# Two neighbouring products of a block change places in TensorE's order

## The chip, the cores and the metric

The kernel runs on one core of a Trainium2 chip. The metric is the device time of one execution in microseconds (us); a kernel's time is the median of its runs.

## The reference

Linear attention with decay over two batches of eight heads, 768 positions and 64 values a head, then two MLPs without bias, one after the other, on the 1536 tokens by 512 values that the attention leaves. All of it in float32:

```
h = x @ w_in                      # 512 -> 2048
g = h * clip(h + 3, 0, 6) / 6     # first MLP;  second MLP: max(0.01 * h, h)
x = g @ w_out                     # 2048 -> 512
```

## The kernel before, in words

The 1536 tokens are three **tiles** of 512 (t = 0, 1, 2). The 2048 hidden values of an MLP are sixteen **slices** of 128 (f = 0 to 15). The work of an MLP is cut into steps (l, b, t, f): MLP, block, tile, slice. `BLOCKS` says how many slices a block has: 1, 3, 4, 4, 4 in the first MLP. Within a block the kernel goes through tile 0 with all slices, then tile 1, then tile 2.

A number is held as a high and a low part (`wh`, `wl`; `xh`, `xl`; `Gh`, `Gl`), and each product is three matmuls: high by high, high by low, low by high.

- **First product** (`gemm1`, L610, called by `one`): 12 matmuls give h of one tile and one slice in a PSUM bank (`h`, of which there are two, for the slices of the first two blocks; `a`, also two, for later ones).
- **Gate** (`gates`): ScalarE L619 (ReLU), VectorE L623 (the product with h, which frees the bank), ScalarE L629 (`Gh`), VectorE L636 (`Gl`).
- **Second product** (`gemm2`, L698): G times the slice of `w_out`, four quarters e = 0 to 3 of 3 matmuls each, summed over the slices of the block in the PSUM banks `acc0` to `acc3` (tile 1 of the first two blocks uses `a` for e = 0 and 1).
- **Collection** of the four banks when a block's last slice of a tile is through (`collect`): in the first MLP's second and third blocks, e = 0, 1 and 2 are copied by ScalarE to a staging buffer `st` (L709), and GpSimd issues a DMA that adds it to the sums in SBUF (L653); e = 3 is added by VectorE (L711). There are two `st` buffers, so the third copy waits until the first of these DMAs has landed, and the bank `acc2` is held until that copy is done.

Weights come in as raw 64-bit values, 512 KB for one slice of one matrix (DMA issued by SyncE, L158; three buffers `raw`). ScalarE (L495, L499) and VectorE (L506 to L521) make float32 of them, ScalarE L527 the high part, VectorE L531 the low part. L518 reads `raw` last, and a new load starts when it is through.

From the third block on, tiles 0 and 1 and two neighbouring slices are multiplied by seven products (`product`, L786, 6 matmuls each) in place of eight, from sums of weights (`s`) and sums of tokens (`T1` to `T4`). Their results are kept and joined by ScalarE L827 and VectorE L831; the join L831 of the third result also frees the second of the two `h` banks.

All operations are entered with `add`, each with what it comes after, which buffers it takes and frees, an assumed duration for each engine and a due time. `Order.issue` walks through assumed time and starts whatever is ready, the one with the lowest due time first, when its engine and buffers are free; this fixes the order of the instructions on each engine for good. First products have due times `due1`, a step of 5.45 apart in the order of the steps; each one is also entered as coming after the one that was entered before it (`prev1`). On the chip, each engine works through its fixed order and waits on semaphores.

Of the kernel before, what the change touches and what calls it, by code (L numbers as in the profile page):

```python
# [131 lines left out]
def decay_attention_two_mlps(ctx: ExitStack, tc: tile.TileContext, qkk, vv, lam, w1, w2, out):  # L132
# [33 lines left out]
    starts = [[sum(bs[:i]) for i in range(len(bs) + 1)] for bs in BLOCKS]  # L166
# [5 lines left out]
    at_step = {(l, t, f): s for s, (l, b, t, f) in enumerate(steps)}  # L172
# [12 lines left out]
    due1 = [T_FIRST + T_STEP * s for s in range(NS)]  # L185
# [162 lines left out]
    def scores_bank(u, g):  # L348
        def fn(e):
            PA["s", u, g] = new("pair", [P, 2, HG, SBT], F32)  # L350
            scores(u, g)(e)
        return fn
# [57 lines left out]
    for u in range(NSB):  # L410
        d, last = DUE_S + SBT_STEP * u, u + 1 == NSB
# [5 lines left out]
    def piece(name, fn, **kw):  # L417
        pieces[name] = add(("pe", PE_US[name[0]]), fn, due_pe[name], **kw)
        return pieces[name]
# [8 lines left out]
    for u in range(NSB):  # L428
        d, last = DUE_S + SBT_STEP * u, u + 1 == NSB
# [11 lines left out]
        for g in range(2):  # L441
            s = piece(("s", u, g), scores_bank(u, g), after=[ld["q", u], ki, op_warm], takes=["pair"])
# [438 lines left out]
    def second_end(ss):  # L881
        nonlocal prev2

        def go(s, e, at, n=None):
            nonlocal prev2
            l, b, t, f = steps[s]
            first, last = f == starts[l][b], f + 1 == starts[l][b + 1]
            bank = "h" if n else f"acc{e}"
            prev2 = add(("pe", 0.68 if n is None else 0.34), gemm2(s, e) if n is None else gemm2_half(s, n), at,
                        after=[gate[s][0], w_ready[l, f, 1], prev2], takes=[bank] * first)  # L890
            if not last:
                return
            cs = slice(0, TT) if n is None else half_of(n)
            c = add(("dve", 0.69 if n is None else 0.42), collect(s, e) if n is None else collect_half(t, n), at,
                    after=[prev2, *taken[t, e]])
            add(("dma", 0.75), store(t, e, cs), at, after=[c])

        places = [(e, None) for e in range(3)] + [(3, 0), (3, 1)]
        for s in ss[:2]:
            for e, n in places:  # L900
                go(s, e, due2[s], n)
            add(("none", 0.0), nothing, after=[prev2], frees=["G", "w1"])
        for group in (places[:2], *([x] for x in places[2:])):
            for s in ss[2:]:
                for e, n in group:
                    go(s, e, due2[ss[3]], n)

    n1, n0 = starts[0][SINGLE] * NTT, NS // 2
# [43 lines left out]
    def one(s, after):  # L952
        nonlocal prev1
        l, b, t, f = steps[s]
        h = "a" if paired(l, f) else "h"
        g1 = add(("pe", 2.73), gemm1(s), due1[s], after=[w_ready[l, f, 0], prev1, *after],
                 takes=[h] + ["G"] * (h == "h"), frees=["w0"] * (t == NTT - 1 and h == "h"))
        last1[l, t] = prev1 = g1
        pieces["m", s] = g1
        gates(s, [g1], h)  # L960
        return g1
# [74 lines left out]
    def seconds(l, b):  # L1036
        for s in range(NS):
            if ends(s):
                continue
            if steps[s][:2] == (l, b):  # L1040
                if steps[s][2] == 2 and steps[s][3] == starts[l][b] and l == 0 and b + 1 == len(BLOCKS[0]):
                    sums_pair()
                sums = second(s, gate[s][0], [gate[s][1]] + ["w1"] * (steps[s][2] == NTT - 1))
                if sums and b + 1 == len(BLOCKS[l]):
                    sums_of[l, steps[s][2]] = sums
        if (l, b) == (1, len(BLOCKS[1]) - 1):
            second_end([s for s in range(NS) if ends(s)])

    x_of = lambda t: [x_ready[c] for c in range(t * SPT, (t + 1) * SPT)]
    for b in range(SINGLE):  # L1050
        for s in range(n1):
            if steps[s][1] == b:
                one(s, x_of(steps[s][2]))
        seconds(0, b)
# [191 lines left out]
```

## Time and profile before

| | before |
|---|---|
| median of 3 runs | 553.12 us (552.95 to 554.85) |
| the profiled execution | 553.77 us |
| its span, first to last instruction | 552.0 us |
| TensorE busy | 543.7 us, 98% of the span |
| VectorE busy | 421.6 us, 76% |
| ScalarE busy | 347.2 us, 63% |
| mean of all DMA | 106 GB/s |

The profiled execution has 1.8 us outside its span, and is 0.65 us above the median. Shares of busy time are means over stages that differ: VectorE is busy 19.48 of the 20 us from 60 to 80, and 164.34 of the 246 us from 300 to 546. The granted TensorE clock is 1.00 in every stretch.

### The profile page before, as it was taken

The numbers are of one execution on the slowest core, as the hardware profiler recorded it, in microseconds if no ns is written. First come the engines' busy times: TensorE is split into PE (matmuls) and PEld (weight loads), VectorE is DVE, ScalarE is ACT, GpSimd is POOL, SyncE is SP. The second block draws the span as 40 slices with busy tenths as digits, with TensorE's granted clock in tenths as the row PEclk, the third lists the DMA queues.
The fourth block names the chain that finished last, engine by engine and source line by source line (L and its number), as shares of the span: only waits on it lengthen the run. The fifth ranks groups of instructions, "written<-read, shape, count | busy, mean of one in ns | idle before, by whom it ended". The sixth has DMA issues, their size and how long they took to land.

```text
span 552.0 us, 8352 instructions
## 1 busy us (share of the span) xinstructions
PE 543.7 (98%) x3174; PEld 457.0 (83%) x3174; DVE 421.6 (76%) x711; ACT 347.2 (63%) x629; POOL 55.7 (10%) x62
## 2 busy tenths in 40 slices
PE   9899999999999999999999999999999999999996
PEld 5788878888888888888888888888888888888885
DVE  4778999899898986888789798786477953883342
ACT  3766976578567754587767796686258735574220
POOL 1680001110110100110000000000110110010000
PEclk9999999999999999999999999999999999999999
DMA  8993333545455323432210411341333522321323
GB/s 284 354 329 143 113 117 57 125 113 145 86 124 172 78 58 86 106 127 64 78 39 1 126 65 44 110 154 38 77 76 115 148 63 53 84 53 23 77 66 88
DMA packets 22571, 58.75 MB, mean 106 GB/s; under 512 B 2690, under 2 KB 2946, under 8 KB 22530
## 3 DMA queue, kind: packets, MB, share of 16 engines
q1 hardware_dynamic: 16944, 48.24, 26.7%
q0 software_dynamic: 5184, 9.44, 10.2%
q8 instruction: 25, 0.41, 0.3%
q10 hardware_dynamic: 402, 0.52, 0.3%
q14 instruction: 16, 0.13, 0.1%
HBM read 45.61 MB, written 3.15 MB: 88 GB/s over the span
## 4 chain that ended last, share of the span: by engine, by line
PE 90%; DMA 5%; DVE 2%; ACT 1%; SPq 0%; issue 0%; ACTq 0%
PE acc L698 45%; PE h L786 21%; PE a L786 14%; PE h L610 5%; DMA sums<-qkk 4%; PE a L610 2%; PE a L698 1%; DMA qk<-qkk 1%; PE pair L345 1%; PE h L395 1%; SPq L158 0%; DVE x_spare L772 0%; ACT ki L318 0%; PE a L387 0%; PE h L387 0%
## 5 line engine op out<-in xcount | busy, mean ns | idle before, releaser
L653 POOL DMA_DIRECT2D sums<-st x36 | 31.8, 933 | 422.0 <-ACT st L709 416.5
L698 PE MATMUL acc<-Gh,wh 128*128 128x512 f32 x136 | 53.1, 390 | 0.0
L698 PE MATMUL acc<-Gl,wh 128*128 128x512 f32 x136 | 53.1, 390 | 0.0
L698 PE MATMUL acc<-Gh,wl 128*128 128x512 f32 x136 | 52.9, 389 | 0.0
L698 PE MATMUL acc<-wh,Gh 128*128 128x512 f32 x124 | 48.5, 391 | 0.0
L698 PE MATMUL acc<-wl,Gh 128*128 128x512 f32 x124 | 48.5, 391 | 0.0
L698 PE MATMUL acc<-wh,Gl 128*128 128x512 f32 x124 | 48.2, 389 | 0.0
L495 ACT ACTIVATE c<-raw 128x512 uint32<-128x512 uint32 x64 | 43.1, 675 | 7.1 <-DVE t L521 5.1
L521 DVE CUSTOM_DVE_ANT_0 t<-t,c 128x1024 uint16<-128x1024 uint16 x64 | 44.3, 692 | 2.2
L711 DVE TENSOR_TENSOR sums<-acc,sums 128x512 f32<-128x512 f32 x35 | 24.1, 690 | 28.3 <-PE acc L698 28.1
L531 DVE TENSOR_TENSOR wl<-t,wh 128x512 fp32r<-128x512 f32 (+1 forms) x64 | 41.9, 659 | 4.0 <-ACT wh L527 3.9
L518 DVE SCALAR_TENSOR_TENSOR t<-raw,t 128x512 uint32<-128x512 uint32 x64 | 44.0, 688 | 1.0
L499 ACT ACTIVATE t<-raw 128x512 f32<-128x512 f32 x64 | 42.8, 668 | 0.0
L527 ACT CAST wh<-t 128x512 fp32r<-128x512 f32 (+1 forms) x64 | 37.7, 591 | 3.0 <-PE acc L698 2.3
L786 PE MATMUL h<-xh,s 128*128 128x512 f32 x112 | 38.4, 389 | 0.0
L506 DVE TENSOR_SCALAR t<-t 128x512 f32<-128x512 f32 x64 | 27.0, 422 | 12.9 <-ACT t L499 12.9
L639 DVE TENSOR_TENSOR Gl<-u,Gh 128x512 fp32r<-128x512 f32 x32 | 22.1, 690 | 17.8 <-ACT Gh L836 17.5
L842 ACT ACTIVATE u<-a 128x512 f32<-128x512 f32 x24 | 14.4, 598 | 29.1 <-PE a L786 29.1
L709 ACT COPY st<-acc 128x512 f32<-128x512 f32 x34 | 19.8, 586 | 18.5 <-PE acc L698 16.2
L698 PEld LDWEIGHTS acc<-Gh,wl 128*128 128x128 f32 x136 | 25.5, 188 | 5.4
L698 PEld LDWEIGHTS acc<-Gh,wh 128*128 128x128 f32 x136 | 25.6, 188 | 4.9
L698 PEld LDWEIGHTS acc<-Gl,wh 128*128 128x128 f32 x136 | 25.6, 188 | 4.9
(210 smaller groups left out, 1478.0 us busy)
## 6 DMA issues: line engine op xcount, KB each, us to landing
raw<-w SPq DMA_DIRECT2D x58, 512.0 KB, 3.3
sums<-st POOLq DMA_DIRECT2D x36, 256.0 KB, 3.8
sums<-qkk SPq DMA_DIRECT2D x12, 256.0 KB, 4.8
vs<-vv SPq DMA_DIRECT2D x12, 256.0 KB, 5.2
sums<-qkk SPq DMA_DIRECT2D x6, 512.0 KB, 5.6
raw<-w SPq DMA_DIRECT2D x12, 256.0 KB, 4.0
out<-sums SPq DMA_DIRECT2D x19, 128.0 KB, 2.4
qk<-qkk SPq DMA_DIRECT2D x4, 512.0 KB, 5.7
```

The costliest lines, as they stand in the source:

```text
L495: nc.scalar.activation(out=CV[h][1], in_=RAW[h][:, :, 0], func=AF.Copy, scale=2.0 ** -29)
L499: return lambda _: nc.scalar.activation(out=CV[h][0].bitcast(F32), in_=RAW[h][:, :, 1].bitcast(F32), func=AF.Abs)
L506: nc.vector.tensor_scalar(out=t.bitcast(F32), in0=t.bitcast(F32), scalar1=MAG_MIN, scalar2=MAG_MAX, op0=ALU.max, op1=ALU.min)
L518: nc.vector.scalar_tensor_tensor(out=t, in0=RAW[h][:, :, 1], scalar=0xC0000000, in1=t, op0=ALU.bitwise_and, op1=ALU.bitwise_or)
L521: nc.vector.tensor_tensor(out=t, in0=t, in1=c, op=ALU.add)
L527: nc.scalar.copy(out=W[h][0][:, cols(*h)], in_=CV[h][0].bitcast(F32)[:, cols(*h)])
L531: return lambda e: eng[e].tensor_tensor(out=W[h][1][:, cols(*h)], in0=CV[h][0].bitcast(F32)[:, cols(*h)], in1=W[h][0].bitcast(F32)[:, cols ...
L610: mm(ps, a[:, ws], x[:, k, :], start=(n == 0), stop=(n == 3 * KC - 1))
L653: return lambda _: nc.gpsimd.dma_start(out=SUM[t][:, e, :], in_=STAGE[t, e], accum_op=ALU.add)
L698: mm(ACC[e], a, x, start=(first and n == 0 and not seeded(s, e)), stop=(last and n == 2), skip_group_check=seeded(s, e))
L711: nc.vector.tensor_tensor(out=acc, in0=ps, in1=acc, op=ALU.add)
L786: mm(ps, ws[a][:, c * P:(c + 1) * P], xs[b][:, c], start=(first and n == 0), stop=(n == 5), skip_group_check=True)
```

## The change

Before the first products of the first two blocks are entered, their list is altered: the step of tile 1 and the block's first slice (l, b, t, f = 0, 1, 1, 1) goes ahead of the step of tile 0 and the block's third slice (0, 1, 0, 3). The due times of first products are dealt out anew to the list, so that the moved step gets the place and the due time of the other. Second products keep their due times and the order in which they are entered.

```
     x_of = ...
+    turns = list(range(n1))
+    other_tile, third_slice = at_step[0, 1, starts[0][1]], at_step[0, 0, starts[0][1] + 2]
+    turns.insert(turns.index(third_slice), turns.pop(turns.index(other_tile)))
+    for s, d in zip(turns, [due1[s] for s in range(n1)]):
+        due1[s] = d
...
     for b in range(SINGLE):
-        for s in range(n1):
+        for s in turns:
             if steps[s][1] == b:
                 one(s, x_of(steps[s][2]))
         seconds(0, b)
```

No instruction is added or taken away: TensorE has the same matmuls. The order differs on TensorE, VectorE and ScalarE from here into the fourth block; behind that it is the same.

On TensorE at the place of the edit, behind the first product of tile 0 and the second slice (its last matmuls are the first three rows; `xh_120` is tile 0, `xh_122` is tile 1), there stood the second products of the block's first slice:

```order
L610 MATMUL h<-xh_120,wh 128x512
L610 MATMUL h<-xl_121,wh 128x512
L610 MATMUL h<-xh_120,wl 128x512
L698 MATMUL acc_1006<-Gh,wh 128x512
L698 MATMUL acc_1006<-Gl,wh 128x512
```

and there stands now the first product of tile 1 and the first slice:

```order
L610 MATMUL h<-xh_120,wh 128x512
L610 MATMUL h<-xl_121,wh 128x512
L610 MATMUL h<-xh_120,wl 128x512
L610 MATMUL h<-xh_122,wh 128x512
L610 MATMUL h<-xl_123,wh 128x512
```

The second products follow it, and then comes the first product of tile 0 and the third slice, one first product later than before.

On TensorE at the start of the fourth block, the second products of its first slice (e = 0 is `acc_2112`, e = 1 is `acc_2119`) were followed by the second of the seven products of the next pair (`T10h`):

```order
L698 MATMUL acc_2119<-Gh,wh 128x512
L698 MATMUL acc_2119<-Gl,wh 128x512
L698 MATMUL acc_2119<-Gh,wl 128x512
L786 MATMUL h<-T10h,s 128x512
L786 MATMUL h<-T10l,s 128x512
```

Now e = 2 (`acc_2125`, in the bank `acc2`) stands between e = 1 (`acc_2111`) and that product; before, e = 2 came four products later:

```order
L698 MATMUL acc_2111<-Gh,wl 128x512
L698 MATMUL acc_2125<-Gh,wh 128x512
L698 MATMUL acc_2125<-Gl,wh 128x512
L698 MATMUL acc_2125<-Gh,wl 128x512
L786 MATMUL h<-T10h,s 128x512
```

On ScalarE at the same place, these rows stood behind the second staging copy of the third block's last tile, and the last of them is the third staging copy, which frees `acc2`:

```order
L629 ACTIVATE Gh<-u 128x512
L527 CAST wh<-t 128x512
L1098 CAST x<-x 128x512
L827 COPY a<-h 128x512
L499 ACTIVATE t<-raw 128x512
L619 ACTIVATE u<-ux,three 128x512
L1098 CAST xh_124<-x 128x2x256
L827 COPY ux<-h 128x512
L629 ACTIVATE Gxh<-u 128x512
L827 COPY ux<-h 128x512
L1098 CAST x<-x 128x512
L709 COPY st<-acc_1923 128x512
```

Now the three staging copies stand so, the third with six rows ahead of it behind the second:

```order
L709 COPY st<-acc_1905 128x512
L495 ACTIVATE c<-raw 128x512
L709 COPY st<-acc_1913 128x512
L629 ACTIVATE Gh<-u 128x512
L499 ACTIVATE t<-raw 128x512
L527 CAST wh<-t 128x512
L827 COPY a<-h 128x512
L495 ACTIVATE c<-raw 128x512
L499 ACTIVATE t<-raw 128x512
L709 COPY st<-acc_1954 128x512
```

On VectorE at the same place, L518, behind which the next weight load starts, stood ahead of the gate L623, and the join L831 was three rows behind the collection L711:

```order
L518 SCALAR_TENSOR_TENSOR t<-raw,t 128x512
L521 ISA t<-t,c 128x1024
L531 TENSOR_TENSOR wl<-t,wh 128x512
L756 TENSOR_TENSOR x<-x 128x512
L623 SCALAR_TENSOR_TENSOR u<-u,h 128x512
L756 TENSOR_TENSOR x<-x 128x512 x2
L711 TENSOR_TENSOR sums<-acc_1929,sums 128x512
L636 SCALAR_TENSOR_TENSOR Gl<-u,Gh 128x512
L531 TENSOR_TENSOR wl<-t,wh 128x512
L831 TENSOR_TENSOR ux<-h,ux 128x512
```

Now L518 stands behind L623, and the join is five rows behind L711:

```order
L623 SCALAR_TENSOR_TENSOR u<-u,h 128x512
L518 SCALAR_TENSOR_TENSOR t<-raw,t 128x512
L521 ISA t<-t,c 128x1024
L711 TENSOR_TENSOR sums<-acc_1962,sums 128x512
L636 SCALAR_TENSOR_TENSOR Gl<-u,Gh 128x512
L756 TENSOR_TENSOR x<-x 128x512
L531 TENSOR_TENSOR wl<-t,wh 128x512
L756 TENSOR_TENSOR x<-x 128x512
L831 TENSOR_TENSOR ux<-h,ux 128x512
```

## Rows read from the trace of the kernel before

**Rows 1.** The page: busy time, share of the span and instructions of each engine
```profile
PE 543.7 (98%) x3174; PEld 457.0 (83%) x3174; DVE 421.6 (76%) x711; ACT 347.2 (63%) x629; POOL 55.7 (10%) x62
```

**Rows 2.** Busy time by stretch: stretch, length, PE, PEld, DVE, ACT, POOL, clock, DMA
```profile
80.00:180.00 100.00, 100.00 (x443) 82.78 (x442) 91.18 (x151) 69.33 (x115) 13.21 (x15) 1.00 0.48 119
180.00:200.00 20.00, 20.00 (x89) 16.25 (x88) 19.72 (x35) 14.38 (x25) 2.59 (x3) 1.00 0.31 67
200.00:546.00 346.00, 345.93 (x1765) 295.69 (x1764) 247.01 (x426) 209.11 (x375) 15.99 (x18) 1.00 0.28 77
```

**Rows 3.** TensorE's timeline, second block: start, duration, operation, idle before it
```profile
71.36 0.39 PE L610 MATMUL h<-xh,wh 128*128 128x512 f32 x1
71.58 0.39 PE L610 MATMUL h<-xl,wh 128*128 128x512 f32 x1
72.20 0.50 PE L610 MATMUL h<-xh,wl 128*128 128x512 f32 x1 [0.23 <-DVE wl L531]
72.53 0.39 PE L610 MATMUL h<-xh,wh 128*128 128x512 f32 x1
...
74.60 0.39 PE L698 MATMUL acc<-Gh,wh 128*128 128x512 f32 x1
```

**Rows 4.** VectorE's timeline, the low parts of two slices' weights
```profile
71.46 1.29 DVE L531 TENSOR_TENSOR wl<-t,wh 128x512 fp32r<-128x512 f32 x2
```

**Rows 5.** TensorE's timeline, end of the third block and start of the fourth
```profile
182.04 0.39 PE L698 MATMUL acc<-Gh,wh 128*128 128x512 f32 x1
...
187.25 0.39 PE L698 MATMUL acc<-Gh,wl 128*128 128x512 f32 x1
187.60 0.50 PE L786 MATMUL h<-T10h,s 128*128 128x512 f32 x1
...
194.55 0.39 PE L786 MATMUL h<-xh,s 128*128 128x512 f32 x1
```

**Rows 6.** ScalarE's timeline at the same place
```profile
182.24 0.69 ACT L619 ACTIVATE u<-h,three 128x512 f32<-128x512 f32 x1 [0.96 <-PE h L786]
182.92 0.59 ACT L709 COPY st<-acc 128x512 f32<-128x512 f32 x1
...
186.32 0.57 ACT L827 COPY a<-h 128x512 f32<-128x512 f32 x1 [0.21 <-PE h L786]
186.80 0.67 ACT L499 ACTIVATE t<-raw 128x512 f32<-128x512 f32 x1
...
191.67 0.59 ACT L709 COPY st<-acc 128x512 f32<-128x512 f32 x1
```

**Rows 7.** VectorE's timeline at the same place
```profile
185.06 0.68 DVE L711 TENSOR_TENSOR sums<-acc,sums 128x512 f32<-128x512 f32 x1
...
186.86 0.69 DVE L831 TENSOR_TENSOR ux<-h,ux 128x512 f32<-128x512 f32 x1
```

**Rows 8.** GpSimd's and SyncE's timelines: an adding DMA, and the weight load before it
```profile
183.91 0.87 POOL L653 DMA_DIRECT2D sums<-st  x1 [17.54 <-ACT st L709]
...
181.35 0.33 SPq L158 DMA_DIRECT2D raw<-w  x1
```

**Rows 9.** The staging tile's view of the adding DMA issued at 183.91
```profile
DMA to landing us min/median/max: 3.3/3.3/3.3
```

**Rows 10.** Another adding DMA, and the weight load issued nearest to it
```profile
L653 POOL DMA_DIRECT2D sums<-st x1: 859/859/859, 165.5 to 165.5; - x1
...
DMA to landing us min/median/max: 5.4/5.4/5.4
...
166.10 0.33 SPq L158 DMA_DIRECT2D raw<-w  x1
```

**Rows 11.** A third adding DMA, and the weight load issued nearest to it
```profile
L653 POOL DMA_DIRECT2D sums<-st x1: 862/862/862, 125.5 to 125.5; - x1
...
DMA to landing us min/median/max: 4.6/4.6/4.6
...
125.27 0.33 SPq L158 DMA_DIRECT2D raw<-w  x1
```

**Rows 12.** The page's DMA issues: count, KB each, median us from issue to landing
```profile
sums<-st POOLq DMA_DIRECT2D x36, 256.0 KB, 3.8
```

## The prediction

> **What bounds the kernel now.** I read the busy times first: TensorE 543.7 us of a span of 552.0, VectorE 421.6, ScalarE 347.2 [rows 1]. A busy share alone does not say that nothing waits, so I read the stretches next: from 80 to 180 us TensorE is busy 100.00 of 100, from 180 to 200 it is busy 20.00 of 20, and from 200 to 546 it lacks 0.07 [rows 2]. The clock is 1.00 throughout. So TensorE sets the time, its work is the same after the change, and all that a new order can do is to remove or make waits of TensorE. The step between matmuls is the yardstick: from 182.04 to 187.25 there are 23 steps [rows 5], 0.2265 us each. A first product of 12 matmuls then takes 2.72, a product of the seven 1.36, and a quarter of a second product 0.68.
>
> Looked at with that step, the second block has one wait. The first product of tile 0 and the third slice starts at 71.36, its third matmul is held for the low part of the weights until 72.20, and its last step ends at 74.60 [rows 3]. VectorE worked on that low part from 71.46 [rows 4]. In the fourth block, the step to the second of the seven products (187.25 to 187.60) is longer than 0.23 as well.
>
> **The edit itself: 0.52 us gained.** The product took 74.60 - 71.36 = 3.24 us where 2.72 are its work, so 0.52 are lost there. In the new order tile 1's product fills the place. It uses the first slice's weights, which tile 0 has used already, and tokens that the first block has used. The third slice's product begins 2.72 later, at 74.08. The rows ahead of its low part on VectorE do not move, so the low part is there at about 72.2, 1.9 us early. I take the whole 0.52 as gained. This is also the bound: apart from it TensorE has little to give from 80 to 546 [rows 2].
>
> **The order behind it: where the wait goes.** The moved step draws a reshuffle behind it, up to the fourth block. Most of it lies where TensorE is fed early; VectorE has 9 us of 100 free from 80 to 180 [rows 2]. One place is close by the order alone: the start of the fourth block, where e = 2 now comes before the `T10` product. I count from the first matmul of the second products of the third block's last tile (182.04 before, "0").
>
> When TensorE wants `acc2`: those second products 2.72, the first of the seven products 1.36, e = 0 and 1 of the next slice 1.36. That is +5.44. Before, e = 2 came four products later, at 187.60 + 5.44 = 193.04 or more, +11.
>
> When `acc2` is free: after the third staging copy. It needs a staging buffer, so the first adding DMA must have landed. GpSimd issued that DMA at 183.91, +1.87 [rows 8], behind the first copy at 182.92 [rows 6], and none of this moves against the second products. It landed after 3.3 us [rows 9], so +5.17. The copy takes 0.59 [rows 6], and a hand-over about 0.05 (the join ended at 187.55 [rows 7], TensorE went on at 187.60 [rows 5]). From the DMA alone: 5.17 + 0.05 + 0.59 + 0.05 = +5.86, a wait of 0.42.
>
> ScalarE's own queue is later than that. The L827 copy follows the first of the seven products and began at 186.32, +4.28; the next operation began 0.48 later [rows 6]. In the new order L495 and L499 follow it and then the third staging copy. An L499 lasts 0.67 and operations overlap by 0.09 (186.32 + 0.57 - 186.80), so 0.58 each: the copy begins at +5.92, ends at +6.51, and TensorE goes on at +6.56. That is a wait of 1.12, with the DMA landing in anything up to 4.0.
>
> Now the DMA. Before, the weight load nearest to it was issued at 181.35, 2.56 us ahead of it [rows 8]. In the new order L518, which gives its buffer free, stands behind the gate L623, which needs the ReLU pass that began at +0.20 and took 0.69 [rows 6]. With VectorE's step of 0.60 (185.06 to 186.86 are three steps [rows 7]) L518 starts at about +1.50, and with some 0.69 of work, as other VectorE operations of this shape, the load is issued at about +2.2 to +2.3, 0.4 behind the adding DMA. Such neighbours are in the trace: with a load issued 0.6 behind it an adding DMA landed after 5.4 us [rows 10], with a load 0.2 to 0.3 ahead after 4.6 [rows 11]; the median of all 36 is 3.8 [rows 12]. I take 4.6, since the order of issue lies between the two and 5.4 stands far above the median. TensorE then goes on at 1.87 + 4.6 + 0.69 = +7.16, a wait of 1.72. With 5.4 it is 2.52, with 3.8 or less 1.12.
>
> The Trainium skill, page "DMA: Bandwidth & Descriptors", section "Issuing engines are not separate DMA queues", says that DMAs started from SyncE, ScalarE and GpSimd end up on the same 16 DMA engines and interleave there. By that rule the load is not free for the adding DMA although another engine issues it, and the dearer end of the wait applies; were the two apart, the cheaper would. The trace agrees, with 3.3 and 5.4 [rows 9, 10].
>
> Behind the wait for `acc2` another is hidden. The `T10` product needs the join L831 [rows 7], which now follows L711 by five steps in place of three. L711 began at +3.02; five steps are 3.00, the join takes 0.69, the hand-over 0.05: +6.76. TensorE would be there at +6.12. If `acc2` were free in time, TensorE would still wait 0.64 here.
>
> From 182.04 to 194.55 [rows 5] there are 54 steps, 12.23 us of 12.51, so 0.28 was lost before, and this is replaced. After a wait the next step was 0.33 in place of 0.23 (72.20 to 72.53 [rows 3]), so 0.10 comes on top. Sum: -0.52 + 1.72 + 0.10 - 0.28 = **+1.02 us**. The profiled execution (553.77) would be 554.8; it lies 0.65 above the median of 553.12, and against the median the forecast is **554.1 us**, +0.2%. That is within 0.5% (2.8 us), about what a measurement of this kernel can tell from no change: I forecast no change.
>
> A second close place is in the second block: tile 1's e = 2 comes 2.72 + 1.36 + 2.72 = 6.80 behind the start of tile 0's last second products, since a first product no longer stands between. By the same prices `acc2` is free at +5.86 with 3.3, at +7.16 with 4.6. At the median, 3.8, it is +6.36: I take nothing, and up to 0.46 for the range (0.36 and the slow step).
>
> **The rivals.**
>
> *The gain stays.* Neither wait arises: -0.52 - 0.28 = -0.80, 552.3 us. For it speaks that TensorE has hardly waited anywhere, so the other engines are mostly early. Against it, the copy can't be done before the landing, which alone gives 0.42. Chance 0.08.
>
> *A small wait.* The DMA lands in under 4.0, as one did in 3.3 [rows 9], because the load comes at another moment. Then the join (0.64) or ScalarE's queue (1.12) decides: -0.52 - 0.28 + 0.10 + 0.64 = -0.06, up to +0.42; 553.1 to 553.5 us. Chance 0.25.
>
> *Slower, by the adding DMA.* At 5.4 the sum is +1.82, 554.9 us. To be slower by over 0.5% the wait has to be 2.77 + 0.52 + 0.28 - 0.10 = 3.47, so the DMA would have to land after 5.44 + 3.47 - 1.87 - 0.69 = 6.35 us. The longest in the trace is 5.4, with one weight load beside it [rows 10]; a load that overlaps it for longer would have to add another microsecond. Chance beyond that point 0.06.
>
> *The edit removes nothing.* If VectorE or ScalarE fell behind because tile 1's gate comes in early, the third slice's product would wait again, by what 1.9 us of margin leave over. The gain of 0.52 goes: about 1.54 above before, 554.7 us. Chance 0.06.
>
> **How the numbers follow.** The likeliest, a wait of 1.12 to 2.52 with the gain kept, has 0.55: 553.5 to 554.9. The range leaves out the case of the whole gain and most of what is beyond 5.4 us and the second close place (+1.82 + 0.46 = +2.28): 552.6 to 555.4. Faster by over 0.5% would need more waiting time than TensorE has: 0.02. Slower by over 0.5% takes the late DMA: 0.06. The same: 0.92.
>
> **What would show it.** In the second block TensorE's third-slice product should step evenly from its first matmul to its last, with no wait for the low part. At the start of the fourth block a wait of 1 to 2.5 us should stand ahead of an L698 matmul, released by ScalarE's L709, and the adding DMA ahead of it should land after over 4 us with a weight load some 0.4 behind its issue. From there TensorE should run about 1 us later than before, to the end. I am wrong if no such wait is there, if another stands in the second or third block that is longer, or if the end moves by other than the sum of the waits.

## The result and the profile after

| | before | changed kernel |
|---|---|---|
| median | 553.49 us (552.95 to 554.85, 4 runs) | 558.11 us (556.92 to 558.89, 4 runs) |
| ratio | | 1.0070, 95% interval 1.0052 to 1.0089 |
| the profiled execution | 553.77 us | 556.92 us |
| its span | 552.0 us | 555.1 us |
| first matmul of the MLPs to the last one, start to start | 503.84 us | 507.83 us |

The kernel is slower by 0.7%, where 554.1 us and no change were forecast. (The ratio is an estimate from all runs; the two medians as they stand give 1.0083, which lies in its interval.) The last row of the table is the gauge for what follows. What comes ahead of the first matmul of the MLPs is not touched by any kernel here and ends at 42.6 to 45.3 us, differently in each profile; in the stretch behind it TensorE sets the time, and this stretch is 3.99 us longer. Its ends stand in TensorE's timelines, first of the kernel before:

```profile
43.57 0.50 PE L610 MATMUL h<-xh,wh 128*128 128x512 f32 x1
...
547.41 0.28 PE L674 MATMUL h<-wh,Gl 128*128 128x256 f32 x1
```

and of the changed kernel:

```profile
42.79 0.50 PE L610 MATMUL h<-xh,wh 128*128 128x512 f32 x1
...
550.62 0.28 PE L674 MATMUL h<-wh,Gl 128*128 128x256 f32 x1
```

**Where the 3.99 us are.** The windows of the changed kernel (the columns of [rows 2]):

```profile
80.00:180.00 100.00, 100.00 (x443) 82.81 (x442) 92.10 (x153) 67.42 (x112) 13.22 (x15) 1.00 0.46 113
180.00:200.00 20.00, 17.11 (x68) 13.65 (x68) 15.73 (x28) 13.53 (x24) 2.59 (x3) 0.91 0.40 93
200.00:550.00 350.00, 349.92 (x1785) 299.07 (x1784) 251.51 (x435) 210.99 (x378) 15.99 (x18) 1.00 0.28 76
```

Only the stretch from 180 to 200 differs from before: TensorE lacks 2.89 us, and the clock is 0.91. Cut finer, the columns being the same:

```profile
185.00:190.00 5.00, 2.11 (x9) 1.43 (x9) 3.22 (x6) 3.12 (x6) 0.41 (x1) 1.00 0.83 184
190.00:191.00 1.00, 1.00 (x4) 0.75 (x3) 1.00 (x3) 1.00 (x3) 0.45 (x1) 0.50 0.07 16
191.00:192.00 1.00, 1.00 (x4) 0.81 (x3) 1.00 (x3) 0.36 (x1) 0.00 (x0) 0.50 1.10 186
192.00:193.00 1.00, 1.00 (x3) 0.75 (x3) 0.96 (x3) 0.15 (x1) 0.00 (x0) 0.50 0.43 72
193.00:194.00 1.00, 1.00 (x5) 0.80 (x4) 0.58 (x1) 0.97 (x2) 0.00 (x0) 0.79 0.02 4
194.00:195.00 1.00, 1.00 (x6) 0.84 (x5) 1.00 (x2) 0.45 (x1) 0.00 (x0) 1.00 0.00 0
```

First TensorE stands idle, then it works at half its clock for three microseconds and more. A busy share shows nothing of the second part: from 190 us on TensorE is "busy" 1.00 of each stretch, but from 190 to 193 with three or four matmuls a microsecond in place of six. TensorE's timeline shows both, and answers to [rows 5]:

```profile
180.74 0.39 PE L698 MATMUL acc<-Gh,wh 128*128 128x512 f32 x1
...
185.95 0.39 PE L698 MATMUL acc<-Gh,wl 128*128 128x512 f32 x1
189.24 0.50 PE L698 MATMUL acc<-Gh,wh 128*128 128x512 f32 x1 [2.89 <-ACT st L709]
189.57 0.40 PE L698 MATMUL acc<-Gl,wh 128*128 128x512 f32 x1
189.81 0.45 PE L698 MATMUL acc<-Gh,wl 128*128 128x512 f32 x1
190.05 0.63 PE L786 MATMUL h<-T10h,s 128*128 128x512 f32 x1
190.48 0.63 PE L786 MATMUL h<-T10l,s 128*128 128x512 f32 x1
...
193.04 0.57 PE L786 MATMUL h<-T20l,s 128*128 128x512 f32 x1
193.45 0.62 PE L786 MATMUL h<-T20h,s 128*128 128x512 f32 x2
```

From 185.95 to 189.24 is 3.29 in place of a step of 0.23: a wait of 3.06. The step behind it is 0.33, which is 0.10 more. From 190.05 to 193.45 there are eight steps of 0.425, 1.59 more than eight of 0.2265. The edit's gain of 0.52 is there too, in the second block, where [rows 3] had the wait for the low weights: the third slice's product now steps evenly, 2.72 from its first matmul to the next product's.

```profile
73.30 0.39 PE L610 MATMUL h<-xh,wh 128*128 128x512 f32 x1
73.53 0.39 PE L610 MATMUL h<-xl,wh 128*128 128x512 f32 x1
73.75 0.39 PE L610 MATMUL h<-xh,wl 128*128 128x512 f32 x1
...
76.02 0.39 PE L698 MATMUL acc<-Gh,wh 128*128 128x512 f32 x1
```

Sum: -0.52 + 3.06 + 0.10 + 1.59, less the 0.23 that the two uneven steps from 187.25 and 187.60 cost before [rows 5]: +4.00, where 3.99 were measured. The second of these steps ends, before, at

```profile
187.94 0.39 PE L786 MATMUL h<-T10l,s 128*128 128x512 f32 x1
```

**What the wait is for.** ScalarE's timeline at that place answers to [rows 6], GpSimd's and SyncE's to [rows 8], and the staging tile's view of the DMA issued at 182.61 to [rows 9]:

```profile
186.08 0.66 ACT L499 ACTIVATE t<-raw 128x512 f32<-128x512 f32 x1
188.60 0.58 ACT L709 COPY st<-acc 128x512 f32<-128x512 f32 x1 [1.86 <-DMA sums<-st]
```

```profile
182.61 0.87 POOL L653 DMA_DIRECT2D sums<-st  x1 [12.93 <-ACT st L709]
...
183.03 0.33 SPq L158 DMA_DIRECT2D raw<-w  x1
...
183.65 0.86 POOL L653 DMA_DIRECT2D sums<-st  x1 [0.17 <-issue]
```

```profile
DMA to landing us min/median/max: 5.9/5.9/5.9
```

The third staging copy had ScalarE free at 186.74 and began at 188.60, when the first adding DMA had landed: 182.61 + 5.91. A weight load had gone out 0.42 us behind that DMA. So the chain is the one that was forecast, with a DMA that took 5.9 us where 4.6 were taken, and with a fall of the clock that stood in no term.

### The profile page after: what moved, and what is told of

It is laid out like the page before. It is cut to its first block, busy times and chain, and to the rows that moved or that the text cites. A ratio compares the mean times of both kernels' runs of the same rounds, so it can differ in the third digit from the quotient of the medians.

```text
span 555.1 us, 8352 instructions
## 1 busy us (share of the span) xinstructions
PE 544.7 (98%) x3174; PEld 458.1 (83%) x3174; DVE 422.4 (76%) x711; ACT 347.6 (63%) x629; POOL 56.2 (10%) x62
## 4 chain that ended last, share of the span: by engine, by line
PE 88%; DMA 7%; issue 3%; ACT 1%; SPq 0%; DVE 0%; POOL 0%; ACTq 0%; POOLq 0%
PE acc L698 44%; PE h L786 20%; PE a L786 14%; PE h L610 6%; DMA sums<-qkk 4%; DMA qk<-qkk 2%; PE a L610 2%; DMA sums<-st 1%; PE a L698 1%; ACT ki L318 0%; SPq L158 0%; PE pair L345 0%; PE h L395 0%; PE h L674 0%; PE acc L674 0%
## 5 line engine op out<-in xcount | busy, mean ns | idle before, releaser
L698 PE MATMUL acc<-Gh,wh 128*128 128x512 f32 x136 | 53.2, 391 | 2.9 <-ACT st L709 2.9
L698 PE MATMUL acc<-Gl,wh 128*128 128x512 f32 x136 | 53.1, 390 | 0.0
L698 PE MATMUL acc<-Gh,wl 128*128 128x512 f32 x136 | 53.0, 389 | 0.0
L698 PE MATMUL acc<-wl,Gh 128*128 128x512 f32 x124 | 48.5, 391 | 0.0
L698 PE MATMUL acc<-wh,Gh 128*128 128x512 f32 x124 | 48.4, 391 | 0.0
L698 PE MATMUL acc<-wh,Gl 128*128 128x512 f32 x124 | 48.2, 389 | 0.0
L711 DVE TENSOR_TENSOR sums<-acc,sums 128x512 f32<-128x512 f32 x35 | 24.1, 690 | 28.2 <-PE acc L698 28.2
L518 DVE SCALAR_TENSOR_TENSOR t<-raw,t 128x512 uint32<-128x512 uint32 x64 | 44.0, 688 | 1.0
L499 ACT ACTIVATE t<-raw 128x512 f32<-128x512 f32 x64 | 42.8, 668 | 0.0
L698 PEld LDWEIGHTS acc<-Gh,wh 128*128 128x128 f32 x136 | 25.6, 188 | 8.2 <-ACT st L709 3.3
L709 ACT COPY st<-acc 128x512 f32<-128x512 f32 x34 | 19.9, 586 | 18.2 <-PE acc L698 12.9
L698 PEld LDWEIGHTS acc<-Gh,wl 128*128 128x128 f32 x136 | 25.5, 188 | 5.4
L698 PEld LDWEIGHTS acc<-Gl,wh 128*128 128x128 f32 x136 | 25.6, 188 | 4.8
```

What stands on the lines that cost most here:

```text
L499: return lambda _: nc.scalar.activation(out=CV[h][0].bitcast(F32), in_=RAW[h][:, :, 1].bitcast(F32), func=AF.Abs)
L518: nc.vector.scalar_tensor_tensor(out=t, in0=RAW[h][:, :, 1], scalar=0xC0000000, in1=t, op0=ALU.bitwise_and, op1=ALU.bitwise_or)
L698: mm(ACC[e], a, x, start=(first and n == 0 and not seeded(s, e)), stop=(last and n == 2), skip_group_check=seeded(s, e))
L711: nc.vector.tensor_tensor(out=acc, in0=ps, in1=acc, op=ALU.add)
```

## The experiments

My theory: the adding DMA is late because the weight load goes out beside it; its landing sets the wait for `acc2`; and the clock falls because of that wait. Rivals: ScalarE's own queue sets the wait; the second adding DMA makes the first one late; the wait is there because the engines reach the fourth block at other times; the fall has nothing to do with the wait; and the edit itself costs time in the second block.

All runs, with the length from the first to the last matmul of the MLPs in the profile, against 503.84 of the kernel before:

| run | length, us | against before | wait at the start of the fourth block, us | clock behind it | time against before, 95% |
|---|---|---|---|---|---|
| e2_third_buffer | 504.27 | +0.43 | 0.93 | 1.00 | 1.0000 (0.9986 to 1.0014) |
| e3_load_later | 506.47 | +2.63 | 2.96 | 1.00 | 1.0059 (1.0038 to 1.0079) |
| e5_edit_alone | 504.32 | +0.48 | none | 1.00 | 0.9995 (0.9983 to 1.0008) |
| e6_rest_alone | 508.28 | +4.44 | 2.75 | 0.50 | 1.0064 (1.0043 to 1.0085) |
| e3b_load_held | 504.53 | +0.69 | 0.93 | 1.00 | 1.0017 (1.0004 to 1.0029) |
| e7_after_again | 507.94 | +4.10 | 2.97 | 0.50 | 1.0076 (1.0057 to 1.0095) |
| e9_edit_and_buffer | 503.70 | -0.14 | none | 1.00 | 1.0003 (0.9989 to 1.0018) |
| e4_copies_5 | 508.36 | +4.52 | 3.39 | 0.50 | one execution |
| e1_quarter_late | 504.43 | +0.59 | 1.07, for L831 | 1.00 | 1.0008 (0.9996 to 1.0020) |
| e4_copies_3 | 505.56 | +1.72 | 2.15 | 1.00 | one execution |
| e3_again | 507.77 | +3.93 | 2.77 | 0.50 | one execution |

The waits are those that the trace puts down to a releaser; the matmul ahead of them is still "busy" for 0.16 us behind its step, so the time lost is that much more (3.06 for 2.89).

### A third staging buffer

```diff
-  tc.tile_pool(name=n, bufs=sizes[n], ...)
+  tc.tile_pool(name=n, bufs=sizes[n] + (n == "st"), ...)
```

The planner goes on counting two, so the order on every engine stays.

> The staging pool gets a third buffer; every engine's order is that of the changed kernel. The third staging copy then waits for no DMA. If the landing of the first adding DMA sets the wait of 3.2 us for acc2, the copy now begins when ScalarE is through with L499 (+6.0 behind the start of the third block's last second products, where TensorE wants the bank at +5.44): +6.0 + 0.58 + 0.05 = +6.63, a wait of about 1.2. If the granted clock fell because TensorE stood idle for that long, it stays at 1.00 here, and the eight slow steps (1.6 us) go as well: 3.2 - 1.2 + 1.6 = 3.6 us below the changed kernel, 0.5 to 1 us above the kernel before. Rival, ScalarE's queue sets the wait: it stays at 3 us, and the time is that of the changed kernel. Rival, the clock falls for another reason: the wait shrinks to 1.2, the clock still falls to 0.50 near 190 us, 2 us below the changed kernel.

ScalarE's timeline and TensorE's in this run:

```profile
186.98 0.66 ACT L499 ACTIVATE t<-raw 128x512 f32<-128x512 f32 x1
187.54 0.58 ACT L709 COPY st<-acc 128x512 f32<-128x512 f32 x1
...
188.17 0.50 PE L698 MATMUL acc<-Gh,wh 128*128 128x512 f32 x1 [0.93 <-ACT st L709]
```

The first adding DMA took 5.7 us here too, but nothing waits for it: the copy follows L499 without a pause, and 1.09 us are lost in place of 3.06. The clock stays at 1.00, and the 1.59 go as well. That ScalarE's queue sets the wait of 3.06 is ruled out (it sets the 1.09 that stay), and that the fall has nothing to do with the wait is unlikely.

### The weight load away from the adding DMA

The first try made the load of the slice (0, 14, 0) wait for the third staging copy in the planner too. The planner then gave its place to the load of (0, 15, 0), so a load still went out 0.42 behind the adding DMA: the run says nothing on its question. It is told because of its clock.

> Two staging buffers as in the changed kernel, the same order on TensorE, VectorE, GpSimd and SyncE; only the weight load that was issued 0.4 us behind the first adding DMA is held back until the third staging copy is done. If that load makes the adding DMA late (5.9 us), it lands after 3.3 to 3.9 us here, ScalarE's queue decides, and the wait is 0.9 to 1.3 us with the clock at 1.00: about 3.5 us below the changed kernel. Rival, the second adding DMA, issued 1.0 us behind the first, makes it late: the first lands after 5.5 to 6 us as before, wait 3, clock falls, time as the changed kernel. In either case the held load's weights come some 5 us later; if they are then needed at once, a new wait for weights shows later in the fourth block and takes part of the gain.

The landing was 6.0 and the wait 2.96, as in the changed kernel, but the clock stayed at 1.00 behind it. The second try holds the load itself and leaves every order as it is; the load that `behind_copy[0]()` issues is made to wait for the copy `c`:

```diff
+                if h == (0, 14, 0):
+                    behind_copy.append(lambda a=a: load(raw[:, a], w[:, a]))
...
-                nc.scalar.copy(out=STAGE[t, e], in_=ps)
+                c = nc.scalar.copy(out=STAGE[t, e], in_=ps)
+                if (s, e) == (23, 2):
+                    behind_copy[0]()
...
```

> The run before it on this question exchanged two weight loads in place of holding one back, so a load still went out 0.42 us behind the first adding DMA. Here that load itself is issued only when the third staging copy is done; every engine's order is the changed kernel's. If the load makes the adding DMA late, the first one lands after 3.3 to 3.9 us in place of 5.9, ScalarE's queue decides, and the wait for acc2 is 0.9 to 1.2 us with the clock at 1.00: the end stands 3.2 to 3.6 us earlier, against the first matmul of the MLPs, than in the profile of the changed kernel. Rival, the second adding DMA, 1.0 us behind the first, makes it late: landing 5.5 to 6 us and a wait of 2.9, as there. The held weights come 5 us later; if a wait for them shows later, it takes part of the gain.

The staging tile's view of the first adding DMA, and TensorE's timeline (L701 is L698, L712 is L709):

```profile
DMA to landing us min/median/max: 3.3/3.3/3.3
```

```profile
190.05 0.50 PE L701 MATMUL acc<-Gh,wh 128*128 128x512 f32 x1 [0.93 <-ACT st L712]
```

With the second adding DMA still 1.04 us behind, the first lands after 3.27 us, as the one before [rows 9]. The weight load alone makes it late by 2.6 us, and the second adding DMA does not. Shown. The length is 0.26 above that of e2; most of this is lost in two uneven steps of TensorE from 128.65 to 129.31 us, long before the held load. It is the same chain at the end of the second block: an adding DMA that landed after 5.8 us holds the third staging copy there.

```profile
128.33 0.59 ACT L712 COPY st<-acc 128x512 f32<-128x512 f32 x1 [1.28 <-DMA sums<-st]
```

The Trainium skill, page "DMA: Bandwidth & Descriptors", section "SWDGE vs HWDGE vs iDMA", says that DMAs issued by GpSimd and those issued by SyncE feed different queues of the same 16 engines, and that each engine takes turns between them. The trace agrees in that beside each other both are late, the adding DMA with 5.9 us in place of 3.3 and the load with 4.2, where the median of 58 loads of this size is 3.3; that they take turns, no trace here shows. The changed kernel's view of that load, and the line of its page for all loads of 512 KB:

```profile
DMA to landing us min/median/max: 4.2/4.2/4.2
...
raw<-w SPq DMA_DIRECT2D x58, 512.0 KB, 3.3
```

### The edit without what follows it, and what follows without the edit

The planner runs twice, once with the new list and once with the old. One order is issued up to 112 us of its assumed time, the end of the second block, and the rest of the work in the order of the other. The diff is that of e5; e6 has the two the other way round.

```diff
-  od.issue()
...
+  head, tail = new_order, old_order
+  done = [o for o in head if o[0] < 112]
+  seen = {n for _, n, _ in done}
+  for _, n, e in done + [o for o in tail if o[1] not in seen]:
+      ops[n][1](e)
```

> The changed kernel's order up to the end of the second block, the order of the kernel before from there on, on every engine: the edit without the reshuffle behind it. If the place at the fourth block's start is all that the change costs, nothing waits for acc2 there, the clock stays at 1.00, and TensorE keeps the 0.52 us of the second block to the end: 0.5 us below the kernel before, which is within what the measurement tells from no change (0.5%). Rival, tile 1's early product itself costs time on VectorE or ScalarE in the second or third block: a wait of over 1 us shows there, and the time is 1 us or more above the kernel before.

> The order of the kernel before up to the end of the second block, the changed kernel's order from there on: the reshuffle without the edit. If the cost lies in the order at the fourth block's start, the wait for acc2 is there with 2.5 to 3.5 us, the clock falls to 0.50 behind it, and the second block's wait for the low weights (0.5 us) is back: 4.6 + 0.5 = about 5 us above the kernel before. Rival, the wait arises because the engines reach the fourth block at other times after the edit: no such wait, and a time within 1 us of the kernel before.

e6: the second block waits for the low weights again, and the fourth block's place costs what it costs in the changed kernel (2.75, with a landing of 5.8, and the clock at 0.50). So the place is made by the order alone, and the edit has no other part in it. The length is +4.44, 0.45 more than the changed kernel's.

e5: no wait at the fourth block, as expected, and 0.53 gained in the second. But from 113 to 128 us it loses 1.0 again, which I had not expected. ScalarE's timeline, then TensorE's (L710 is L709, L828 is L827):

```profile
122.67 0.64 ACT L630 ACTIVATE Gh<-u 128x512 fp32r<-128x512 f32 x1
124.64 0.59 ACT L710 COPY st<-acc 128x512 f32<-128x512 f32 x1 [1.33 <-DMA sums<-st]
...
126.31 0.59 ACT L828 COPY a<-h 128x512 f32<-128x512 f32 x1
...
126.95 0.50 PE L787 MATMUL h<-T20h,s 128*128 128x512 f32 x1 [0.26 <-ACT a L828]
```

It is the same chain at the end of the second block: an adding DMA that landed after 5.4 us holds the third copy and all that stands behind it on ScalarE. Whether the buffers are the cause, the next run says; its edit is the two above together.

> The edit without the reshuffle behind the second block, as before, and a third staging buffer with the same order on every engine. The edit alone gained 0.51 us in the second block and lost 0.94 between 115 and 128 us, where the third copy of the second block's last tile waited 1.33 us for an adding DMA that landed after 5.4, and ScalarE's copy of a product came late behind it. If the staging buffers are the cause there as well, TensorE keeps its gain: 0.5 us below the kernel before against the first matmul of the MLPs, no wait of over 0.1 us between 110 and 200. Rival, ScalarE is late there by its own queue: the loss of 0.4 to 0.9 us stays. By the time alone, 0.1%, neither can be told from no change.

The copy then begins without a pause at 124.14, and the 0.6 at 127 us are gone. Some 0.4 stay, in two uneven stretches at 115 and 118 us, behind ScalarE's L828 and VectorE's L832. In all -0.14 us: the best of all lengths, and by time the same as the kernel before (1.0003). The expectation of -0.5 was too high.

### How long a wait, and the clock

With three buffers the third copy is done several times over (the output stays), so that a wait of any length is made without waiting for a DMA. The diff is that of e4_copies_5; e4_copies_3 has 3.

```diff
-  nc.scalar.copy(out=STAGE[t, e], in_=ps)
+  for _ in range(5 if (s, e) == (23, 2) else 1):
+      nc.scalar.copy(out=STAGE[t, e], in_=ps)
```

> Three staging buffers, the changed kernel's order, and the third staging copy of the third block's last tile done five times in place of once (the output is the same): an idle time of TensorE that no DMA sets, 0.93 + 4 x 0.53 = 3.0 us. If the length of the idle time alone makes the clock fall, it falls to 0.50 behind it, as behind 2.9 in the changed kernel; if the DMA traffic has a part in it or the length isn't all, the clock may stay at 1.00.

> Three staging buffers and the third staging copy done three times (the output is the same): done five times it gave an idle time of 3.4 us and the clock fell behind it, done once 0.9 and it stayed. Three times should give 0.93 + 2 x 0.6 = 2.1 us. If an idle time of any length above some bound between 0.9 and 2.75 brings the clock down, this halves the bracket; the end stands 1.2 us behind the run with one copy if it stays at 1.00, 2.8 if it falls.

> The changed kernel once more, beside the experiments. The wait for acc2 should be 2.7 to 3.0 us again with a landing of 5.7 to 6.0. The open question is the clock: behind an idle time of 2.9 and of 2.75 us it fell to 0.50, behind one of 2.97 in another kernel it did not. If the length alone decides, it falls here as in the first profile. If something else has a part in it, it may stay at 1.00, and the end then stands 1.6 us earlier against the first matmul of the MLPs.

> The kernel with two weight loads exchanged, once more, for the clock alone: an idle time of 2.97 us was not followed by a fall in its first profile, while one of 2.97 in the changed kernel was. If the execution decides and not the kernel, the clock may fall here; if this kernel's order of loads keeps the clock up, it stays at 1.00 again. Wait for acc2 2.9 to 3.0 in either case.

The windows from 180 to 200 us and the waits in TensorE's timeline, of e4_copies_3:

```profile
180.00:200.00 20.00, 17.85 (x79) 14.44 (x78) 17.86 (x31) 16.27 (x30) 2.59 (x3) 1.00 0.48 116
```

```profile
190.40 0.50 PE L698 MATMUL acc<-Gh,wh 128*128 128x512 f32 x1 [2.15 <-ACT st L710]
```

of e4_copies_5:

```profile
180.00:200.00 20.00, 16.61 (x67) 13.19 (x66) 15.26 (x27) 15.34 (x28) 2.59 (x3) 0.91 0.47 116
```

```profile
191.59 0.50 PE L698 MATMUL acc<-Gh,wh 128*128 128x512 f32 x1 [3.39 <-ACT st L710]
```

and of the two executions of one kernel, e3_load_later and e3_again (L704 is L698, L715 is L709):

```profile
180.00:200.00 20.00, 17.04 (x76) 13.74 (x75) 17.08 (x30) 14.40 (x26) 2.59 (x3) 1.00 0.44 104
```

```profile
190.48 0.50 PE L704 MATMUL acc<-Gh,wh 128*128 128x512 f32 x1 [2.96 <-ACT st L715]
```

```profile
180.00:200.00 20.00, 17.23 (x69) 13.74 (x68) 15.71 (x28) 13.38 (x24) 2.59 (x3) 0.91 0.40 93
```

```profile
189.67 0.50 PE L704 MATMUL acc<-Gh,wh 128*128 128x512 f32 x1 [2.77 <-ACT st L715]
```

Five copies made a wait of 3.39, where 3.0 were expected. In its one execution a wait that ScalarE alone makes brings the clock down as one for a DMA does, so no DMA is needed for the wait. In the changed kernel the fall came again behind 2.97. Behind 0.93 (twice), 1.07 and 2.15 it did not come, behind 2.75, 2.77, 2.89, 2.97 and 3.39 it did, and behind 2.96 in one execution it did not, while the same kernel had it in another behind less. So the length counts, but it doesn't decide alone between 2.7 and 3.0. What decides there stays open. That executions of one kernel differ shows ahead of the MLPs too: from 20 to 35 us the clock was 1.00 in the changed kernel's first profile and 0.89 in e7_after_again.

### The quarter put behind the products

`pair_ops[0, 5][4]` is the fifth of the seven products, behind which the quarter now comes.

```diff
+  if steps[s] == (0, 3, 0, 8) and e == 2:
+      od.ops[prev2][3].append(pair_ops[0, 5][4])
...
```

> The quarter e = 2 of the fourth block's first slice is entered as coming after the fifth of the seven products, so it can't stand ahead of the T10 product; the first of the seven products goes ahead of e = 1, and T10 follows e = 1. Nothing wants acc2 early, so the late adding DMA should cost nothing. What the forecast put behind that wait comes to light: T10 needs the join L831, five VectorE steps behind L711. L711 began 2.92 us behind the start of the third block's last second products in the changed kernel; five steps are 3.0, the join 0.68, the hand-over 0.05: +6.65, where TensorE wants it at +5.44. A wait of 1.2 us, the clock at 1.00: against the first matmul of the MLPs 0.5 us above the kernel before, 3.5 below the changed kernel. Rival, the join is not late because VectorE is itself earlier with nothing waiting: no wait of over 0.3, 0.5 us below the kernel before.

```profile
186.55 0.39 PE L698 MATMUL acc<-Gh,wl 128*128 128x512 f32 x1
188.01 0.50 PE L786 MATMUL h<-T10h,s 128*128 128x512 f32 x1 [1.07 <-DVE ux L831]
```

TensorE's timeline shows the wait that the forecast called hidden: 188.01 - 186.55 - 0.23 = 1.23 us for the join L831, where 1.2 were expected. Here the load went out 1.46 ahead of the adding DMA, which landed after 3.3, so the run does not show whether a late one would cost nothing there, as expected.

## Why the prediction was wrong

**The bound and the gain.** Right. TensorE sets the time, and the edit gives back 0.51 to 0.54 us in the second block in each kernel that has it; e6, which lacks it, has the old wait there.

**The place.** Right, to a tenth. TensorE wanted `acc2` at 185.95 + 0.23 - 180.74 = +5.44, the adding DMA was issued at +1.87, and the load 0.42 behind it where about 0.4 was forecast.

**ScalarE's queue, +6.56, a wait of 1.12.** Right: e2 and e3b lose 1.09 there.

**The hidden join.** Right: e1 meets it at 188.01, which is +6.67 from its second products, where +6.76 was forecast.

**The second close place, taken as nothing.** Right; no wait stands there in any of the profiles. In the changed kernel the adding DMA there, issued at 83.25, landed after 3.5 us.

**The landing. This step failed.** "I take 4.6, since the order of issue lies between the two and 5.4 stands far above the median." It was 5.91. The formula was sound: 1.87 + 5.91 + 0.69 = +8.47, and TensorE went on at +8.50. What went in was wrong. The load's issue 0.4 behind lay near the neighbour 0.6 behind with 5.4 [rows 10], not midway between it and the one ahead [rows 11], and the median of 3.8 [rows 12] is that of 36 landings of which only these two have a load issued within 0.6 us. The longest of the trace was no bound either: with the load closer behind than in any of its rows, the landing was longer than all of them. I had also misread that row: I wrote "with one weight load beside it", but a second load of 512 KB went out 1.19 behind the same adding DMA.

```profile
166.70 0.41 SPq L158 DMA_DIRECT2D raw<-w  x1
```

So the row was not the price of one load 0.6 behind, and no row had that price. With 5.91 the sum would have been -0.52 + 3.03 + 0.10 - 0.28 = +2.33, still 0.4%, within what I called no change, and at the upper end of my range. e3_load_later is that case: a wait of 2.96, the clock at 1.00, +2.63.

**The clock. A term that was missing.** "The clock is 1.00 throughout" was read in the kernel before and carried over to a kernel in which TensorE stands idle for about 3 us, which before it never did between 80 and 546 [rows 2]. The fall cost 1.59 us, and it is what brings the change from 0.4% to 0.7%. The rival "slower, by the adding DMA" had the right mechanism, but asked for a landing beyond 6.35, since it paid for the wait alone.

## What to carry to other kernels

A transfer's landing is priced from rows in which the same neighbour goes out beside it, and where the neighbour follows more closely than in any of these rows, the dearest of them is no upper end: here it was 5.4, and 5.91 was measured. A wait of TensorE of nearly 3 us is not priced by its length: here the slow clock behind it added half as much again. Where a planner with assumed durations sets the order, a change early in the list has to be followed through the order of every engine to the end, and the buffer that holds the new neighbour back (here the second of two staging buffers) is worth more thought than the place of the edit.

## What the hardware showed that I had not expected

The landing of an adding DMA (256 KB) hangs on when a weight load (512 KB) goes out beside it. At the fourth block's start it is 3.3 us in the five profiles where no load is issued within 1.4 us (before, e1, e3b, e5, e9). With a load 0.59 behind and a second one 1.19 behind, it is 5.2 to 5.4 in three profiles; with one 0.39 to 0.43 behind, 22 cases in the changed kernel and the experiments, 5.6 to 6.4, though the load is issued later and by another engine. With the nearest load 0.9 to 1.1 us ahead it lies between 3.9 and 5.8. A load 1.25 to 1.6 ahead leaves the first of two adding DMAs at 3.3 to 3.8; the second of two close ones lands later even with no load issued within 2 us (after 3.8 to 6.2).

The granted clock went from 1.00 to 0.50 not when TensorE stood still but 0.8 us after it had gone on (189.24 to 190.05), and came back after eight matmuls. In the other four falls at this place the first slow step began 0.6 to 1.5 us after TensorE had gone on. At 0.50, the 1.2 GHz level, the matmuls of 512 columns start 0.427 us apart. The Trainium skill, page "TensorE: Matmul & The Clock Gate", section "Wait — 56ns, not 53.3ns?", gives 426.7 ns for such matmuls at the lower clock; the trace agrees.
